# Score products as three float32r passes over halves, with the attention stage in a newly searched order

## The chip, the cores and the metric

The program runs on one core of one Trainium2 chip. The metric is the device time of one execution in microseconds. The kernel before takes 1178.76 us (median of 3 runs, 1177.21 to 1178.91).

## The reference

Attention over 4 x 8 heads of 576 positions with head size 64, where only scores within `tau` of a row's maximum count; then a gated layer on the 2304 x 512 result after RMS normalisation; then a second layer with `h * cos(h)`. Cut to what matters:

```python
scores = scale * np.matmul(q, k.transpose(0, 1, 3, 2))
thresh = np.max(scores, axis=-1, keepdims=True) - tau
scores = np.where(scores >= thresh, scores, -1000000000.0)
attn = np.exp(scores - np.max(scores, axis=-1, keepdims=True))
attn = attn / (np.sum(attn, axis=-1, keepdims=True) + 1e-09)
x = np.matmul(attn, v)                      # then to (2304, 512)

xn = x / np.sqrt(np.mean(x * x, -1) + 1e-06) * rms_g
g = xn @ w_gate
y = (silu(g) * (xn @ w_val)) @ w_out        # 512 -> 1536 -> 512
h = y @ w_in                                # 512 -> 2048
out = (h * np.cos(h)) @ w_out2              # 2048 -> 512
```

## The kernel before

**Three stages.** Attention works on 16 pairs of heads, the gated layer on 6 chunks of 384 tokens by 6 groups of 2 hidden blocks, the second layer on the same chunks by groups of 3 or 2. The two layers multiply in float32r: each operand is split into a rounded half (`hi`) and the remainder (`lo`), and `mm3` (L740) issues three matmuls, hi x hi, hi x lo and lo x hi, into one PSUM bank. Their order is written out in loops.

**A pair of heads in attention.** DMA brings k, q and v. `prep_pe` transposes k and q on TensorE (psb and psc for k, psa for q), `prep_act` copies them from PSUM to SBUF on ScalarE, q with the scale. Then five units follow, four of 128 queries for each of the two heads and a fifth that holds the last 64 queries of both. For a unit `s_mm` (L496) multiplies queries and keys into the PSUM tiles s0 and s1, of which each has one buffer; `s_max` copies them out on VectorE and takes the row extreme, `s_exp` is on ScalarE, `s_thr` on GpSimd, `s_mask` on VectorE, then `t_pe` (pst) and `c_pe` (psc) transpose the weights on TensorE, and `av` multiplies them with v (po). A pair's result is divided by the sums on GpSimd (`av_div`), squared and summed for the RMS (`x_sq`, `x_add`); after every fourth pair `x_sum` (pss, TensorE), `x_mean`, `rms` and `rms_t` make the RMS factor, which SP writes out and reads back spread over the partitions.

**The score products before.** The operands are plain float32. For units 0 to 3 a head's matmul uses 64 of the 128 rows of the array, head 0 the upper and head 1 the lower, so that the two heads' matmuls lie in different row groups; a unit is 2 column halves (288 columns each) x 2 heads, that is 4 matmuls in the program, and the trace shows 8, two for each float32 matmul. The fifth unit uses 64 x 64 tiles, 4 matmuls in the program and 8 in the trace.

**What sets the order.** Attention, with the first four blocks of gate and value products (`gv`, tile pgv) and the first two of output products (`px`) of the gated layer, is ordered by the class `Plan`: a list of steps with an engine, a duration, a place number (`STEPS`, L28), the steps that each follows, and the buffers that it takes and frees. `order` runs through it with one clock per engine and emits at each point the step that can start first by its durations, ties going to the place number. `SIGNAL` (L83) is added until another engine sees a step's end, `SWITCH` when TensorE changes its tile shape (`TILING`, L90). Each engine then works through its list strictly in that order, and so does SP with its DMAs. What comes after `plan.run` is a loop written out by hand; it begins with the third block of `px`, then block 4 of `gv`, and so on.

Of the kernel before, what the change touches and what calls it, by code (L numbers as in the profile page):

```python
# [10 lines left out]
F32R = mybir.dt.float32r  # L11
# [7 lines left out]
P = 128  # L19
# [9 lines left out]
    "none": ("", 0, 989236),  # L29
    "load_k": ("SP", 1700, -2080791, 5000),  # L30
    "load_q": ("SP", 1700, -71929, 7000),
    "load_v": ("SP", 1700, 1092105, 5000),
    "pb": ("PE", 440, -510840),
    "pa": ("PE", 440, -238233),
    "pc": ("PE", 330, 5527),
    "pb_a": ("ACT", 590, -16795),
    "pa_a": ("ACT", 690, -1741191),
    "pc_a": ("ACT", 480, -1089184),
    "s": ("PE", 960, -2067487),
    "s4": ("PE", 490, -536410),  # L40
    "warm": ("PE", 640, -512436),
    "max": ("DVE", 833, -2165065),
    "exp": ("ACT", 785, 18525),
    "th": ("POOL", 300, -79889),
    "mask": ("DVE", 890, -806542),
    "t": ("PE", 438, 45402),
    "raw": ("ACT", 595, -536576),
    "c0": ("PE", 220, -1677441),
    "c1": ("PE", 440, -448255),
    "c_raw": ("ACT", 415, -134803),  # L50
    "radd": ("POOL", 250, 59203),
    "rinv": ("DVE", 430, -724883),
    "r_out": ("SP", 2100, -470089, 2500),
    "r_in": ("SP", 1700, -1508061, 11000),
    "av0": ("PE", 2110, -2836787),
    "av1": ("PE", 2660, -1235121),
    "avo": ("ACT", 420, -1389171),
    "div": ("POOL", 1410, -632364),
    "xout": ("SP", 500, 133651, 2500),
    "sq": ("POOL", 1145, 981189),  # L60
    "x_add": ("POOL", 1410, 831228),
    "xsum": ("PE", 1150, 324869),
    "mean": ("DVE", 150, -1745391),
    "rms": ("POOL", 1520, 218301),
    "rs_out": ("SP", 2500, 1117322, 2500),
    "x_load": ("SP", 500, 404214, 6000),
    "x_p": ("POOL", 1010, 1534732),
    "x_a": ("ACT", 610, 636723),
    "x_d": ("DVE", 550, -11859),
    "jdma": ("SP", 500, 542601, 5000),  # L70
    "j1": ("DVE", 600, -1949661),
    "j2": ("DVE", 690, -1330761),
    "j_p": ("POOL", 1310, 3046632),
    "j_a": ("ACT", 620, -146518),
    "gv": ("PE", 2100, -1185087),
    "silu": ("ACT", 500, -877901),
    "px": ("PE", 2100, 184028),
    "pxc": ("ACT", 500, 1363803),
    "hmul": ("DVE", 560, 68682),
    "hhi": ("ACT", 520, -551420),  # L80
    "hlo": ("DVE", 560, -825852),
}
SIGNAL = 100  # L83
# [6 lines left out]
TILING = {"s": 1, "s4": 3, "av0": 2, "av1": 2}  # L90
# [15 lines left out]
class Plan:  # L106
# [8 lines left out]
    def add(self, kind, at, fn, *args, after=(), take=(), free=()):  # L115
        eng, ns, place, landing = (STEPS[kind] + (SIGNAL if STEPS[kind][0] else 0,))[:4]
# [95 lines left out]
def attention_moe_cos_kernel(  # L212
# [283 lines left out]
    def s_mm(n):  # L496
# [799 lines left out]
```

## Time and profile before

| | us |
|---|---|
| median of 3 runs | 1178.76 |
| the profiled execution | 1178.78 |
| its span | 1176.8 |
| attention up to the first block of pgv on TensorE | 304 |
| TensorE busy | 1162.3 |
| VectorE busy | 791.6 |
| ScalarE busy | 656.8 |
| GpSimd busy | 315.5 |

The profiled execution is within 0.02 us of the median, so that sums can be made against it; 2.0 us lie outside its span. In the profile PE is TensorE's matmuls, PEld its weight loads, DVE VectorE, ACT ScalarE, POOL GpSimd, SP the DMA queue. Matmuls are pipelined and overlap in the rows, so what a matmul costs the engine is read from start to start of the next one, not from its duration.

### The profile page before, as it was taken

What the parts mean: (1) busy time and instruction counts of PE and PEld (TensorE: products, weight loads), DVE (VectorE), ACT (ScalarE), POOL (GpSimd) and SP (SyncE); (2) the same over time, 40 slices, a digit from 0 to 9 for tenths busy, and PEclk for the clock granted to TensorE, in tenths of its full rate; (3) what the DMA queues carried; (4) which work ended last, traced back from release to release, by engine and by line L of the source; (5) the groups of instructions that cost most, each with busy time, mean ns of one, the idle gap of its engine ahead of it and who ended that gap; (6) DMA issues with size and microseconds to landing.
All of it is one profiled execution on the core that took longest, in us unless ns stands there. A gap on an engine that the chain in (4) does not pass through costs nothing.

```text
span 1176.8 us, 18220 instructions
## 1 busy us (share of the span) xinstructions
PE 1162.3 (99%) x6836; PEld 1021.4 (87%) x6836; DVE 791.6 (67%) x1547; ACT 656.8 (56%) x1234; POOL 315.5 (27%) x299
## 2 busy tenths in 40 slices
PE   9999999999999999999999999999999999999997
PEld 7666666666899999999999999999999999999995
DVE  6788777787477463643636439578687796867765
ACT  5888777776445321312313225377677676766663
POOL 1233343333653020100201102014234243332222
PEclk9999999999999999999999999999999999999999
DMA  6454324211543030110301103002112021000014
GB/s 134 118 146 113 89 70 102 56 51 49 152 160 105 19 108 1 54 55 1 108 1 54 54 1 91 18 1 75 34 36 72 1 72 36 27 11 1 1 54 108
DMA packets 99448, 71.66 MB, mean 61 GB/s; under 512 B 65040, under 2 KB 89360, under 8 KB 99360
## 3 DMA queue, kind: packets, MB, share of 16 engines
q1 hardware_dynamic: 98256, 70.20, 21.1%
q8 instruction: 54, 0.88, 0.3%
q10 hardware_dynamic: 1040, 0.26, 0.1%
q14 instruction: 34, 0.28, 0.1%
q0 software_dynamic: 64, 0.03, 0.0%
HBM read 60.95 MB, written 9.52 MB: 60 GB/s over the span
## 4 chain that ended last, share of the span: by engine, by line
PE 92%; issue 3%; ACT 2%; DVE 2%; DMA 0%; POOL 0%; SPq 0%; POOLq 0%; ACTq 0%
PE pgv L742 24%; PE ph L742 16%; PE po L742 16%; PE px L742 12%; PE s L510 8%; PE po L636 7%; PE pst L599 5%; ACT et L609 1%; PE psc L618 1%; PE psa L444 1%; ACT e L549 0%; PE psb L444 0%; PE pss L676 0%; PE warm L708 0%; DVE xl L736 0%
## 5 line engine op out<-in xcount | busy, mean ns | idle before, releaser
L742 PE MATMUL pgv<-xl,whi 128*128 128x384 f32 x576 | 194.5, 338 | 2.3 <-DVE xl L736 2.3
L742 PE MATMUL pgv<-xh,whi 128*128 128x384 f32 x576 | 194.4, 337 | 0.0
L742 PE MATMUL pgv<-xh,wlo 128*128 128x384 f32 x576 | 194.2, 337 | 0.0
L318 POOL TENSOR_TENSOR wtmp<-wtmp,raw 128x512 int32<-128x512 int32 x68 | 93.1, 1369 | 354.8 <-DVE wtmp L314 340.4
L1201 POOL TENSOR_TENSOR hlo<-r,hhi 128x384 fp32r<-128x384 f32 x96 | 98.2, 1023 | 303.6 <-ACT hhi L1200 247.6
L766 ACT ACTIVATE hh<-pgv 128x384 f32<-128x384 f32 x72 | 35.5, 493 | 248.8 <-PE pgv L742 248.8
L770 DVE TENSOR_TENSOR hh<-hh,pgv 128x384 f32<-128x384 f32 x72 | 39.7, 552 | 161.2 <-ACT hh L766 161.2
L742 PE MATMUL ph<-xh,whi 128*128 128x384 f32 x384 | 129.6, 337 | 0.0
L742 PE MATMUL ph<-xl,whi 128*128 128x384 f32 x384 | 129.5, 337 | 0.0
L742 PE MATMUL ph<-xh,wlo 128*128 128x384 f32 x384 | 129.2, 336 | 0.0
L530 DVE TENSOR_SCALAR_CACHE_REDUCE s<-s 128x576 f32<-128x576 f32 x128 | 91.9, 755 | 42.1 <-PE s L510 41.8
L1183 ACT ACTIVATE t<-ph,magic 128x384 f32<-128x384 f32 x96 | 55.8, 582 | 111.5 <-PE ph L742 111.5
L742 PE MATMUL po<-whi,hlo 128*128 128x512 f32 x288 | 114.6, 398 | 1.4 <-POOL hlo L1201 1.4
L742 PE MATMUL po<-whi,hhi 128*128 128x512 f32 x288 | 113.8, 395 | 0.2 <-ACT hhi L1200 0.2
L742 PE MATMUL po<-wlo,hhi 128*128 128x512 f32 x288 | 113.4, 394 | 0.0
L742 PEld LDWEIGHTS pgv<-xl,whi 128*128 128x128 f32 x576 | 108.6, 189 | 3.0 <-DVE xl L736 2.9
L742 PEld LDWEIGHTS pgv<-xh,whi 128*128 128x128 f32 x576 | 108.7, 189 | 0.6 <-issue 0.5
L742 PEld LDWEIGHTS pgv<-xh,wlo 128*128 128x128 f32 x576 | 108.7, 189 | 0.0
L559 DVE SCALAR_TENSOR_TENSOR e<-s,th,e 128x576 f32<-128x576 f32 x128 | 101.0, 822 | 0.5 <-POOL th L540 0.4
L1190 DVE SCALAR_TENSOR_TENSOR r<-t,r 128x384 f32<-128x384 f32 x96 | 99.0, 1032 | 3.3
L549 ACT ACTIVATE e<-s,m 128x576 f32<-128x576 f32 x128 | 95.2, 785 | 4.9 <-DVE s L530 4.8
L742 PE MATMUL px<-hhi,whi 128*128 128x384 f32 x288 | 97.9, 340 | 0.0
(118 smaller groups left out, 2456.5 us busy)
## 6 DMA issues: line engine op xcount, KB each, us to landing
raw<-in_moe_w_out_dram SPq DMA_DIRECT2D x28, 512.0 KB
raw<-in_moe_w_in_dram SPq DMA_DIRECT2D x16, 512.0 KB
raw<-in_moe_w_gate_dram SPq DMA_DIRECT2D x12, 512.0 KB
raw<-in_moe_w_val_dram SPq DMA_DIRECT2D x12, 512.0 KB
x<-xb SPq DMA_DIRECT2D x16, 288.0 KB
kn<-in_k_dram SPq DMA_DIRECT2D x16, 256.0 KB
vn<-in_v_dram SPq DMA_DIRECT2D x16, 256.0 KB
qn<-in_q_dram SPq DMA_DIRECT2D x15, 256.0 KB
```

The lines of the kernel that those rows point to most:

```text
L318: nc.gpsimd.tensor_tensor(tmp, tmp, lw, op=ALU.add)
L510: nc.tensor.matmul(ps[:, c, 0:288], lhs, kh[r, k0:k0 + 288], start=True, stop=True,)
L530: nc.vector.tensor_scalar(s.rearrange("p (c n) -> p c n", c=2), un[n].pop(("ps", hd))[:, :, 0:288], qscale[:, 0:1] if n % 5 == 4 else 1.0, ...
L549: nc.scalar.activation(un[n]["e"][:, hd], un[n]["s", hd], AF.Exp, bias=grp[group_of(n)]["m"][:, c], scale=-1.0)
L559: nc.vector.scalar_tensor_tensor(e, un[n].pop(("s", hd)), grp[group_of(n)]["th"][:, ci:ci + 1], e, op0=ALU.is_le, op1=ALU.mult, accum_out= ...
L599: nc.tensor.transpose(ps[:, c], e[:, hd, k0:k0 + P], ident)
L636: nc.tensor.matmul(po[64 * hd:64 * hd + 64, :], vn[:, c, hd, :] if c < 4 else vl[:, hd, :], hf[j]["et"][:, hd, c, :] if c < 4 else hf[j][" ...
L742: nc.tensor.matmul(ps, w[a], x[bb], start=first and i == 0, stop=last and i == 2)
L770: nc.vector.tensor_tensor(hq[n], hq[n], pgv.pop(n)[:, 1, 0:TC], op=ALU.mult)
L1183: nc.scalar.activation(t, ph, AF.Identity, bias=magic[:, 0:1], scale=INV2PI)
L1190: nc.vector.scalar_tensor_tensor(r, t, -C2, r, op0=ALU.mult, op1=ALU.add)
L1201: nc.gpsimd.tensor_tensor(lo, r, f(hi), op=ALU.subtract)
```

## The change

The score products go from float32 to three float32r passes. `prep_act` now writes the rounded half of q and k; a new step `prep_lo` on VectorE (pa_l, pb_l, pc_l) computes the remainder from the same PSUM tile, three instructions for each pair; `s_mm` runs three passes for each column half: 12 matmuls for units 0 to 3, in alternating row groups as before. The fifth unit is no longer cut into 64 x 64 tiles: the last 64 queries of the two heads are loaded as a block-diagonal 128 x 128 tile, which takes two DMAs instead of one in `load_q`, and one matmul over all 128 rows gives both heads; it has 6 matmuls and TensorE's usual tile shape. There are two tiles each of k and q (a hi and a lo one) where four could be held before. The first unit waits for pair 0's `prep_lo` too.

In the engine model the durations of `STEPS` are new throughout, `SIGNAL` is set for each engine, `s4` has left `TILING`, and the place numbers are new, so that the order of the whole attention stage is another. The instructions after that stage are the same ones in the same order, from the third block of `px` on.

```diff
-    "s": ("PE", 960, -2067487),
-    "s4": ("PE", 490, -536410),
...
+    "pb_l": ("DVE", 605, -2192168),
...
+    "s": ("PE", 885, -3334861),
+    "s4": ("PE", 790, 52577),
...
-SIGNAL = 100
+SIGNAL = {"PE": 190, "DVE": 110, "ACT": 145, "POOL": 60, "SP": 100, "": 0}
...
-TILING = {"s": 1, "s4": 3, "av0": 2, "av1": 2}
+TILING = {"s": 1, "av0": 2, "av1": 2}
...
-        small(p).dma_start(
-            q4[p % 2][0:64].rearrange("p (h d) -> p h d", h=2), rest(q, p).rearrange("h p d -> p h d")
-        )
+        for j in range(2):
+            r = slice(64 * j, 64 * j + 64)
+            small(p).dma_start(q4[p % 2][r, r], rest(q, p)[j])
...
-            qk[nm, p] = f(qk_p.tile([P, w], F32R, tag=nm + ("hi", "lo")[p % 2], name=nm))
+            qk[nm, p] = [qk_p.tile([P, w], F32R, tag=nm + x, name=nm + x) for x in ("hi", "lo")]
...
+    def prep_lo(p, kind):
+        nm = "q" if kind == "a" else "k"
+        c0, c1 = PREP_COLS[kind]
+        hi, lo = (x[:, c0:c1] for x in qk[nm, p])
+        nc.vector.scalar_tensor_tensor(
+            lo, pre.pop((p, kind))[:, 0:c1 - c0], qscale[:, 0:1] if kind == "a" else 1.0, f(hi),
+            op0=ALU.mult, op1=ALU.subtract,
+        )
...
         for c in range(2):
-            for hd in range(2):
-                k0 = 288 * c + (64 if hd and u < 4 else 128)
-                r = slice(64 * hd, 64 * hd + 64)
-                if u == 4:
-                    ps, lhs = un[n]["ps", 0][r], kh[r, 768:832]
-                else:
-                    ps, lhs = un[n]["ps", hd], qk["q", p][r, u * P:(u + 1) * P]
-                nc.tensor.matmul(
-                    ps[:, c, 0:288], lhs, kh[r, k0:k0 + 288], start=True, stop=True,
-                )
+            for i, (a, bb) in enumerate(((0, 0), (0, 1), (1, 0))):
+                for hd in heads(n):
+                    k0 = 288 * c + (64 if hd else 128)
+                    r = slice(0, P) if u == 4 else slice(64 * hd, 64 * hd + 64)
+                    lhs = kh[a][:, 768:896] if u == 4 else qk["q", p][a][r, u * P:(u + 1) * P]
+                    nc.tensor.matmul(
+                        un[n]["ps", hd][:, c, 0:288], lhs, kh[bb][r, k0:k0 + 288],
+                        start=i == 0, stop=i == 2,
+                    )
...
-            "s0": 1, "s1": 1, "t": 3, "v": 1, "k": 4, "q": 4, "kn": 2, "qn": 2, "q4": 2, "vn": 2,
+            "s0": 1, "s1": 1, "t": 3, "v": 1, "k": 2, "q": 2, "kn": 2, "qn": 2, "q4": 2, "vn": 2,
...
-                    ready[p].append(add("p" + kind + "_a", n, prep_act, p, kind, after=[x],
+                    x = add("p" + kind + "_a", n, prep_act, p, kind, after=[x])
+                    ready[p].append(add("p" + kind + "_l", n, prep_lo, p, kind, after=[x],
                         free=[("pre", p, kind)],
                     ))
```

**Where instructions now stand.** First TensorE, in the sixth pair, the last two units: s_ tiles are the score products of head 0 and head 1, pst the transposes of the weights. Before:

```order
217 L510 MATMUL s_1490<-k,q 128x288
218 L510 MATMUL s_1491<-k,q 128x288
219 L510 MATMUL s_1490<-k,q 128x288
220 L510 MATMUL s_1491<-k,q 128x288
221 L599 MATMUL pst<-ident,e 128x128 x8
222 L510 MATMUL s_1517<-k 64x288 x4
```

Now (L520 is the line of the score products, khi, klo, qhi and qlo are the halves; the six matmuls of the unit's first column half stand ahead of these, and three more of the last unit behind):

```order
423 L520 MATMUL s_1671<-khi,qhi 128x288
424 L520 MATMUL s_1672<-khi,qhi 128x288
425 L520 MATMUL s_1671<-klo,qhi 128x288
426 L520 MATMUL s_1672<-klo,qhi 128x288
427 L520 MATMUL s_1671<-khi,qlo 128x288
428 L520 MATMUL s_1672<-khi,qlo 128x288
429 L610 MATMUL pst<-ident,e 128x128 x12
430 L520 MATMUL s_1722<-khi 128x288
431 L520 MATMUL s_1722<-klo,khi 128x288
432 L520 MATMUL s_1722<-khi,klo 128x288
```

The unit of two heads has gone from 4 rows to 12, the fifth unit from 4 rows of 64 x 288 to 6 of 128 x 288, between the same neighbours.

Next VectorE, round the fifth unit's maximum (with qscale) of the third pair; L530 and L541 are the maxima, L559 and L570 the masks, L328 and L331 a weight's low half. Before:

```order
68 L530 TENSOR_SCALAR s,m<-s_787 128x576
69 L530 TENSOR_SCALAR s,m<-s_788 128x576
70 L530 TENSOR_SCALAR s,m<-s_831,qscale 128x576
71 L571 RECIPROCAL r_145<-r_145 128x9
72 L572 STREAM_TRANSPOSE rt<-r_145 128x32
73 L559 SCALAR_TENSOR_TENSOR e,sum<-s,th,e 128x576
74 L328 TENSOR_TENSOR wlo<-wtmp,whi 128x512
75 L559 SCALAR_TENSOR_TENSOR e,sum<-s,th,e 128x576
76 L530 TENSOR_SCALAR s,m<-s_874 128x576
```

Now:

```order
82 L541 TENSOR_SCALAR s,m<-s_944,qscale 128x576
83 L331 TENSOR_TENSOR wlo<-wtmp,whi 128x512
84 L487 SCALAR_TENSOR_TENSOR klo<-psb,khi 128x512
85 L487 SCALAR_TENSOR_TENSOR qlo<-psa,qscale,qhi 128x512
86 L541 TENSOR_SCALAR s,m<-s_987 128x576
87 L541 TENSOR_SCALAR s,m<-s_988 128x576
88 L487 SCALAR_TENSOR_TENSOR klo<-psc,khi 128x384
89 L570 SCALAR_TENSOR_TENSOR e,sum<-s,th,e 128x576
90 L541 TENSOR_SCALAR s,m<-s_1029 128x576
91 L541 TENSOR_SCALAR s,m<-s_1030 128x576
92 L570 SCALAR_TENSOR_TENSOR e,sum<-s,th,e 128x576
```

The three remainders of the next pair's keys and queries (L487) have come in between the maxima.

Last the end of attention. On GpSimd xe is chunk 1 of the next layer's input being scaled, acc chunk 3, and r_149 the power that gives the last RMS factor. Before:

```order
131 L667 TENSOR_TENSOR sq<-sq 128x576
132 L729 TENSOR_TENSOR xe<-xe 128x384 x4
133 L795 TENSOR_TENSOR acc<-acc,rs 128x1536
134 L687 TENSOR_TENSOR r_149<-r_149,expo 128x5
135 L318 TENSOR_TENSOR wtmp<-wtmp,raw 128x512
```

Now:

```order
131 L678 TENSOR_TENSOR sq<-sq 128x576
132 L740 TENSOR_TENSOR xe<-xe 128x384 x4
133 L698 TENSOR_TENSOR r_149<-r_149,expo 128x5
134 L806 TENSOR_TENSOR acc<-acc,rs 128x1536
135 L321 TENSOR_TENSOR wtmp<-wtmp,raw 128x512
```

The power (L687, now L698) stands ahead of the scaling of chunk 3 (L795, now L806), behind which it stood. TensorE at the same place, where pss is the sum of squares for that factor and px the first blocks of output products; before:

```order
700 L742 MATMUL px_4078<-hhi,whi 128x384
701 L742 MATMUL px_4078<-hlo,whi 128x384
702 L742 MATMUL px_4078<-hhi,wlo 128x384
703 L676 MATMUL pss<-ones,sq 128x1 x5
704 L742 MATMUL px_4174<-hhi,whi 128x384
```

Now:

```order
1275 L753 MATMUL pgv<-xh,whi 128x384
1276 L753 MATMUL pgv<-xl,whi 128x384
1277 L753 MATMUL pgv<-xh,wlo 128x384
1278 L687 MATMUL pss<-ones,sq 128x1 x5
1279 L753 MATMUL px_4736<-hhi,whi 128x384
```

The sum stood behind the 24 matmuls of the first two blocks of px and now stands ahead of them, right behind the fourth block of pgv. The last two po steps, which before stood ahead of all pgv, now stand between the second and the third block.

## Rows read from the trace of the kernel before

**Rows 1.** Page, part 1: busy time of each engine, share of the span, instructions.
```profile
PE 1162.3 (99%) x6836; PEld 1021.4 (87%) x6836; DVE 791.6 (67%) x1547; ACT 656.8 (56%) x1234; POOL 315.5 (27%) x299
```

**Rows 2.** Busy us (x instructions) in attention: PE, PEld, DVE, ACT, POOL; clock, DMA.
```profile
20.00:304.00 284.00, 281.19 (x2107) 186.48 (x2103) 223.21 (x614) 221.32 (x402) 102.57 (x116) 1.00 0.35 92
```

**Rows 3.** Waits within 20 to 304: engine line <- releaser, us in total, times, longest.
```profile
DVE s L530 <- PE s L510: 53.2, 65, 2.7
...
PEld s L510 <- DVE e L559: 9.0, 23, 0.5
```

**Rows 4.** PE timeline, unit of undivided queries: start, us, line, tile, xcount.
```profile
151.44 1.24 PE L510 MATMUL s<-k,q 64*128 64x288 f32 x8
152.62 0.44 PE L618 MATMUL psc<-ident,e 128*128 128x128 f32 x2
152.89 0.27 PE L449 MATMUL psb<-ident,k 128*128 128x128 f32 x1
153.00 0.49 PE L444 MATMUL psb<-ident,kn 128*128 128x128 f32 x3
```

**Rows 5.** PE timeline, fifth unit (64 x 64 tiles), and what stands round it.
```profile
165.04 0.60 PE L599 MATMUL pst<-ident,e 128*128 128x128 f32 x4
165.57 1.19 PE L510 MATMUL s<-k 64*64 64x288 f32 x8
166.69 0.49 PE L636 MATMUL po<-et,vn 128*64 128x320 f32 x2
```

**Rows 6.** Weight loads (PEld) and matmuls of one such step, in three windows.
```profile
151.79 0.19 PEld L510 LDWEIGHTS s<-k,q 64*128 64x128 f32 x2
...
152.03 0.19 PEld L510 LDWEIGHTS s<-k,q 64*128 64x128 f32 x2
...
151.79 0.65 PE L510 MATMUL s<-k,q 64*128 64x288 f32 x4
```

**Rows 7.** Groups by line: DVE operations on PSUM and SBUF; xcount, busy us, mean ns.
```profile
L1241 DVE TENSOR_TENSOR acc<-acc,po 128x512 f32<-128x512 f32 x90 | 60.9, 685 | 28.7 <-PE po L742 28.1
...
L1189 DVE SCALAR_TENSOR_TENSOR r<-t,ph 128x384 f32<-128x384 f32 x96 | 52.8, 550 | 61.1 <-ACT t L1184 60.4 <-ACT hhi L1200 0.7
```

**Rows 8.** PE timeline, float32r matmuls of 384 and 512 columns.
```profile
900.93 0.33 PE L742 MATMUL ph<-xh,whi 128*128 128x384 f32 x1
...
901.45 0.40 PE L742 MATMUL po<-whi,hhi 128*128 128x512 f32 x1
...
903.55 0.34 PE L742 MATMUL ph<-xh,whi 128*128 128x384 f32 x1
```

**Rows 9.** DVE's busiest 20 us of attention at a full PE, by stretch.
```profile
80.00:100.00 20.00, 19.96 (x148) 13.15 (x146) 17.28 (x46) 16.37 (x31) 8.34 (x10) 1.00 0.53 141
```

**Rows 10.** PE timeline, first unit of the program: start, us, what, releaser.
```profile
8.39 1.24 PE L510 MATMUL s<-k,q 64*128 64x288 f32 x8 [0.50 <-ACT q L476]
```

**Rows 11.** PE timeline, end of attention's steps and the stall behind it.
```profile
325.17 1.17 PE L676 MATMUL pss<-ones,sq 128*128 128x1 f32 x10
...
354.23 0.43 PE L742 MATMUL pgv<-xh,whi 128*128 128x384 f32 x1
356.43 0.44 PE L742 MATMUL pgv<-xl,whi 128*128 128x384 f32 x1 [1.76 <-DVE xl L736]
```

**Rows 12.** Stretch behind that stall, columns as in the group by stretch above.
```profile
357.10:360.50 3.40, 3.40 (x12) 3.40 (x12) 2.82 (x6) 1.44 (x3) 0.00 (x0) 0.50 0.00 0
```

**Rows 13.** POOL and DVE timelines there: chunk 3 scaled, the power, chunk 4 split.
```profile
326.31 3.50 POOL L795 TENSOR_TENSOR acc<-acc,rs 128x1536 f32<-128x1536 f32 x1
329.76 1.51 POOL L687 TENSOR_TENSOR r<-r,expo 128x5 f32<-128x5 f32 x1
...
355.77 2.19 DVE L736 SCALAR_TENSOR_TENSOR xl<-acc,g_sb,xh 128x384 fp32r<-128x384 f32 x4
```

**Rows 14.** DVE and POOL: the last mask, and the last sum of squares.
```profile
296.65 0.81 DVE L559 SCALAR_TENSOR_TENSOR el<-s,th,el 128x576 f32<-128x576 f32 x1
...
319.31 1.43 POOL L667 TENSOR_TENSOR sq<-sq 128x576 f32<-128x576 f32 x1 [0.82 <-DVE hlo L778]
```

More of the change, by code (lines that the diff above doesn't have):

```diff
@@ L43 @@
[L43 to L81, printed above, removed]
+    "none": ("", 0, 42756),
+    "load_k": ("SP", 1700, -6287439, 5000),
+    "load_q": ("SP", 2300, -583941, 7000),
@@ new lines @@
+    "load_v": ("SP", 1700, 266270, 5000),
+    "pb": ("PE", 440, -860938),
+    "pa": ("PE", 440, -872284),
+    "pc": ("PE", 355, 39154),
+    "pb_a": ("ACT", 477, -1117404),
+    "pa_a": ("ACT", 580, -2512624),
+    "pc_a": ("ACT", 362, -2064268),
+    "pa_l": ("DVE", 605, -2991832),
+    "pb_l": ("DVE", 605, -2192168),
+    "pc_l": ("DVE", 470, -5857582),
+    "s": ("PE", 885, -3334861),
+    "s4": ("PE", 790, 52577),
+    "warm": ("PE", 640, 30908),
+    "max": ("DVE", 680, -4929605),
+    "exp": ("ACT", 675, 1243882),
@@ new lines @@
+    "th": ("POOL", 300, -873324),
+    "mask": ("DVE", 742, -1254623),
+    "t": ("PE", 445, 69130),
+    "raw": ("ACT", 477, -1893158),
+    "c0": ("PE", 245, -2814656),
+    "c1": ("PE", 465, 3616),
+    "c_raw": ("ACT", 295, -1313205),
+    "radd": ("POOL", 250, -463947),
+    "rinv": ("DVE", 375, -2021598),
+    "r_out": ("SP", 2100, -3188116, 2500),
+    "r_in": ("SP", 1700, -348085, 11000),
+    "av0": ("PE", 2212, -5925497),
+    "av1": ("PE", 2745, -2855374),
+    "avo": ("ACT", 300, -133807),
@@ new lines @@
+    "div": ("POOL", 1385, 1088743),
+    "xout": ("SP", 500, 2391295, 2500),
+    "sq": ("POOL", 1122, 1869781),
+    "x_add": ("POOL", 1385, 1123049),
+    "xsum": ("PE", 1085, 246324),
+    "mean": ("DVE", 140, -2146351),
+    "rms": ("POOL", 1520, 1629785),
+    "rs_out": ("SP", 2500, 2224996, 2500),
+    "x_load": ("SP", 500, 2392020, 6000),
+    "x_p": ("POOL", 1010, 1606859),
+    "x_a": ("ACT", 540, 3436637),
+    "x_d": ("DVE", 480, -40858),
+    "jdma": ("SP", 500, 2917392, 5000),
+    "j1": ("DVE", 440, -3496085),
@@ L82 @@
+    "j2": ("DVE", 608, -2428094),
+    "j_p": ("POOL", 1310, 2858989),
+    "j_a": ("ACT", 540, 290309),
+    "gv": ("PE", 2090, -400213),
+    "silu": ("ACT", 420, 2761497),
+    "px": ("PE", 2090, 288516),
+    "pxc": ("ACT", 400, -194883),
+    "hmul": ("DVE", 480, -472662),
+    "hhi": ("ACT", 420, 1595094),
+    "hlo": ("DVE", 480, -4555793),
 }
-SIGNAL = 100
+SIGNAL = {"PE": 190, "DVE": 110, "ACT": 145, "POOL": 60, "SP": 100, "": 0}
 SWITCH = 100
@@ L115, in add @@
     def add(self, kind, at, fn, *args, after=(), take=(), free=()):
-        eng, ns, place, landing = (STEPS[kind] + (SIGNAL if STEPS[kind][0] else 0,))[:4]
+        eng, ns, place, landing = (STEPS[kind] + (SIGNAL[STEPS[kind][0]],))[:4]
         step = {
@@ L852, in attention @@
             prep_act(0, kind)
+            prep_lo(0, kind)
             warm(m)
```

18 lines of the change are left out of this document (3 added, 15 removed).

## Prediction

> **What bounds the kernel now.** The page's first part comes first: TensorE is busy for 99% of the span, VectorE for 67% [rows 1]. Since matmuls overlap in the rows, that share alone proves little, so the stretch of attention comes next: from 20 to 304 us TensorE is busy for 281.2 of 284 us at the full clock, VectorE for 223.2, ScalarE for 221.3 [rows 2]. The list of waits then tells which way the waiting goes: VectorE sits idle for 53.2 us until a score product has ended, while the largest wait of TensorE's weight loads, for a mask on VectorE, comes to 9.0 us in 23 pieces [rows 3]. So attention runs at TensorE's pace, and what a step costs TensorE from start to start counts nearly one for one. The new order ends there too: what follows is the same list of instructions, so nothing but its start and one stall at its beginning can move.
>
> **The score products of two heads.** A unit starts at 151.44 and the next instruction at 152.62, 1.18 us [rows 4]. A transpose in a row takes 0.11 us (152.89 to 153.00) [rows 4]; four of them from 165.04 should end at 165.48, yet the next unit starts at 165.57, so a change of tile shape costs 0.09 us ahead of the step [rows 5]. That makes 1.27 us for a unit. Inside it, one pair of float32 instructions (both heads at once) follows the next at 0.24 us, 151.79 to 152.03 [rows 6]; four pairs are 0.96 us, and 0.31 us are edges, the first weight load and the draining for the other tile shape. The new unit keeps the edges and has 6 pairs in float32r.
>
> A float32r pass of 288 columns is not in the trace. Three of 384 columns take 0.52 us from 900.93 to 901.45, 0.173 each, and nine of 512 take 2.10 us up to 903.55, 0.233 each [rows 8]: 0.451 and 0.456 ns for a column, so proportional, and 0.130 us for 288. The bounds: a pass cannot be cheaper than half a float32 pair, 0.120, and is not dearer than the one of 384 columns, 0.173. I take 0.130, which both sizes give. A unit then costs 6 x 0.130 + 0.31 = 1.09 us, 0.18 less, and 16 x 4 units give 11.5 us.
>
> The Trainium skill, "TensorE: Matmul & The Clock Gate", section "Back-to-back issue gap", states N/2.4 + 2.5 ns for a matmul in a stream. By that a pass would be 122.5 ns, as an estimate, and the whole sum below would come to about 1160.7 us; for 384 columns it says 162.5 ns where the row shows 173, so the trace does not agree.
>
> That the two heads still run at once in float32r is an assumption, and the rows that carry it are those of float32: the loads of both heads are in one piece of 0.19 us at 151.79, x2, in the moment in which the matmuls of the pair before start, 151.79 [rows 6]. Neither the other row group nor a matmul in flight holds the load back.
>
> The same page, Part 3, "The mechanism", says that a weight load overlaps a matmul in flight only where the row group differs; here it would put a load between any two passes. The trace does not agree: the load at 151.79 belongs to the same two row groups as the matmuls that start at 151.79.
>
> **The fifth unit.** It runs from 165.57 to 166.69, 1.12 us, with 0.09 ahead [rows 5], so 1.21. The new one has 6 passes over the full array and TensorE's usual tile shape, so no edges: 0.78 us, 0.43 less, and 6.9 us for 16 pairs. Together TensorE is relieved of **18.4 us**. With passes of 0.120 it would be 23, with 0.173 it would be 2.4 us more work than before.
>
> **What VectorE gets.** Three remainders for each pair, each from PSUM and SBUF. The nearest rows are 685 ns for 512 columns and 550 ns for 384 [rows 7], so 2 x 0.685 + 0.55 = 1.92 us a pair, 28.8 us for the 15 pairs that are prepared behind 20 us. They lie beside TensorE's work as long as they fall into the 53.2 us in which VectorE waits for score products [rows 3]. But s0 and s1 have one buffer each: the next unit's products wait for this unit's maxima, and a remainder that stands ahead of a maximum, as it now does, puts it off by 0.55 to 0.69 us. VectorE's share rises from 79% to about 252 of 271 us, 93%; the highest that I find in 20 us beside a full TensorE is 17.28, 86% [rows 9]. The bounds are nothing and all 28.8 us. I take 5 us, nearer to the lower end, because the idle time is nearly twice the new work and TensorE's waits for VectorE are now only a few us; about one remainder in six then reaches TensorE.
>
> **The beginning.** The first unit starts at 8.39, when ScalarE has written pair 0's operands [rows 10]. Now its last remainder comes behind that, 0.55 us with the row of 384 columns. TensorE waits there for the chain of one unit, so the relief of the first five units and the first fifth one, 5 x 0.18 + 0.43 = 1.3 us, is not on the path either. Together **1.9 us** against the change. The second small load of q4 costs SP or POOL one more issue; the loads run a pair ahead, and I cost it at nothing. If that cover is gone, it is under 1 us for each pair. Two k and q tiles instead of four mean that a pair is prepared right behind the last unit of the pair two before it, still a whole pair (some 17 us) ahead of its use; I cost that at nothing too.
>
> **The end of attention.** The sum for the last RMS factor, pss, starts at 325.17 [rows 11], and chunk 4 of the next layer, which needs the factor, is split from 355.77 on [rows 13]; TensorE waits for it from 354.23 to 356.43 [rows 11], 2.0 us beyond the pace of 0.17. Behind that stall the granted clock is at half, 1.2 GHz, from 357.1 to 360.5 [rows 12], 3.4 us for the work of 1.7. In the new order pss stands ahead of 24 px matmuls (24 x 0.173 = 4.2 us), and the power, 1.51 us, no longer waits for the scaling of chunk 3, 3.50 us [rows 13]. The chain is 7.7 us earlier against TensorE's list, more than the stall, so 3.7 us should go. A new wait may come at pss itself: from the last mask, over at 297.46, to the last sum of squares, over at 320.74 [rows 14], are 23.3 us, with a round trip through DRAM in it, and between them TensorE now has four blocks of pgv (16.6 us), 12 transposes (1.3 us) and two po steps, which is about as much. I take 0.7 us of the 3.7 back and count **3.0 us**.
>
> **The sum,** against the profiled execution of 1178.8, which is also the median: 1178.8 - 18.4 + 1.9 + 5 - 3.0 = **1164.3 us**.
>
> **Rivals.**
> - VectorE becomes the bound. If it cannot be filled beyond the 86.4% of [rows 9], 252 us of work need 252/0.864 = 291.7 us, 7.7 more than the 284 of now: 1178.8 + 7.7 + 0.6 - 3.0 = 1184 us, slower than before. It decides below a share of 252/(284 + 2.4) = 88%. For it speaks that maxima and masks come in bursts and that ScalarE and VectorE work in turns on each unit; against it that VectorE's idle time now is TensorE's doing [rows 3].
> - The heads no longer run at once in float32r. A unit has 12 passes, 1.87 us, 0.60 more: 64 x 0.60 - 6.9 = 31.5 us more, and 1178.8 + 31.5 + 1.9 - 3.0 = 1209 us. If each pass first waited for its load of 0.19 us, a unit would take 6 x 0.32 + 0.31 = 2.23 us and a fifth unit 1.92, 64 x 0.96 + 16 x 0.71 = 72.8 us more, 1250 us in all. Against both stands [rows 6]. (The second is what the rule of Part 3 above would give.)
> - A smaller gain: VectorE costs 12 us instead of 5, or the stall behind attention stays since TensorE waits at pss instead. 1171 and 1167 us, 1174 for both.
> - A larger gain: passes at 0.120 and the wait for VectorE at nothing, 1155 us. (The skill's rule on the gap points this way.)
>
> **How the numbers follow.** About 0.2%, 2.4 us, is what a measurement of this kernel can tell from no change. Chances: 0.60 for the forecast with its own spread of 1157 to 1170; 0.06 for less than that; 0.13 for the smaller gain, 1170 to 1176; 0.06 for within 2.4 us of now; 0.11 for VectorE as the bound and 0.04 for heads one after the other or loads between the passes. That is 0.79 faster, 0.06 the same, 0.15 slower. The range from 1156 to 1180 leaves out both slower rivals and the end of the larger gain, some 0.2.
>
> **What would show it.** In the new profile a unit of two heads should take about 1.0 us from its first matmul to the next instruction, its pairs 0.13 us apart with both heads within 0.01; a fifth unit 0.78 us. If the pairs are 0.26 apart, the second rival holds. VectorE's share of attention should be 90% or more, and TensorE's wait for L541 and L570 some us in total; if attention's part of TensorE's list ends no earlier, the first rival holds. The first pgv of chunk 4 should follow without a stall and the clock should stay at its full level there; a wait at pss would show as idle time ahead of it, for GpSimd's last sum.

## The result

The changed kernel takes **1166.64 us** (median of 4 runs, 1164.42 to 1167.45) against 1178.07 before (4 runs, 1177.21 to 1178.91): a ratio of 0.9904, 95% interval 0.9892 to 0.9916, 11.4 us less. A second group of runs on another occasion gave 1165.91 against 1177.81, 0.9896 (0.9882 to 0.9911). The forecast was 1164.3. The direction, the size and the relief by the products of two heads came out as worked out. The fifth unit's relief was taken too large and the price of VectorE's new work too high, and the two errors nearly cancel. One execution below, of the kernel with one pass, took 2758.64 us, more than twice the others of that kernel, and is left out of its median.

The profiled execution took 1167.45 us with a span of 1165.6. Its page, part 1 (busy us, share of the span, instructions) and part 4 (the chain that ended last, by engine and by line), answer to [rows 1]:

```profile
PE 1145.0 (98%) x7060; PEld 1036.4 (89%) x7060; DVE 817.5 (70%) x1595; ACT 653.2 (56%) x1234; POOL 317.4 (27%) x300
...
PE 86%; DVE 7%; issue 4%; ACT 1%; POOL 1%; DMA 0%; SPq 0%; POOLq 0%; DVEq 0%; ACTq 0%
PE pgv L753 24%; PE ph L753 16%; PE po L753 16%; PE px L753 12%; PE po L647 5%; PE s L520 5%; PE pst L610 4%; DVE s L541 2%; DVE e L570 2%; PE psc L629 1%; DVE klo L487 1%; DVE wtmp L317 0%; DVE wtmp L312 0%; PE pss L687 0%; DMA k<-in_k_dram 0%
```

TensorE is busy 17 us less. VectorE has a larger part of the chain than any engine but TensorE: the maxima (L541), the masks (L570) and the new remainders (L487) stand in it.

Attention by stretch (length, then busy us of PE, PEld, DVE, ACT, POOL; clock, DMA), answering to [rows 2], and the waits from 20 to 288 us, answering to [rows 3]:

```profile
20.00:288.00 268.00, 260.05 (x2266) 199.12 (x2265) 248.79 (x658) 215.30 (x397) 100.08 (x112) 0.99 0.38 98
```
```profile
DVE s L541 <- PE s L520: 12.5, 22, 1.9
PEld s L520 <- DVE s L541: 7.4, 18, 1.4
PE s L520 <- DVE s L541: 4.0, 8, 1.1
```

The first pgv starts at 288.23 instead of 304.01, but that is not the same point: 12 transposes and two po steps, 7.1 us from 296.67 to 303.79, now stand behind the second block. The first mark with the same work ahead of it in both kernels is block 4 of `gv`. Before, then the changed kernel in this trace:

```profile
328.37 0.34 PE L742 MATMUL pgv<-xh,whi 128*128 128x384 f32 x1
```
```profile
319.74 0.34 PE L753 MATMUL pgv<-xh,whi 128*128 128x384 f32 x1
```

It starts 8.6 us earlier here, and 11.6 in a second trace, which has not the half clock shown below. VectorE is busy for 248.79 of 268 us, 93%, and its wait for score products has fallen from 53.2 to 12.5 us. TensorE's loads now wait for maxima for 7.4 us and its matmuls, partly in the same pieces, for 4.0; in [rows 3] the largest such wait, for masks, was 9.0.

A unit of two heads on TensorE (start, us, line, tile, count), answering to [rows 4 and 6]:

```profile
100.36 0.40 PE L520 MATMUL s<-khi,qhi 64*128 64x288 f32 x2
100.59 0.30 PE L520 MATMUL s<-klo,qhi 64*128 64x288 f32 x2
100.73 0.29 PE L520 MATMUL s<-khi,qlo 64*128 64x288 f32 x2
100.86 0.29 PE L520 MATMUL s<-khi,qhi 64*128 64x288 f32 x2
101.00 0.30 PE L520 MATMUL s<-klo,qhi 64*128 64x288 f32 x2
101.13 0.29 PE L520 MATMUL s<-khi,qlo 64*128 64x288 f32 x2
101.35 0.33 PE L629 MATMUL psc<-ident,e 128*128 128x128 f32 x1
```

It takes 0.99 us from its first matmul to the next instruction, with 0.09 ahead 1.08. Each row holds both heads, 3 to 4 ns apart, and behind the first pair, which takes 0.23, the pairs follow each other at 0.13 to 0.14 us. A fifth unit, answering to [rows 5]:

```profile
111.59 0.38 PE L520 MATMUL s<-khi 128*128 128x288 f32 x1
111.80 0.29 PE L520 MATMUL s<-klo,khi 128*128 128x288 f32 x1
...
112.34 0.29 PE L520 MATMUL s<-khi,klo 128*128 128x288 f32 x1
112.47 0.60 PE L610 MATMUL pst<-ident,el 128*128 128x128 f32 x4
```

It takes 0.88 us: its first pass lasts 0.21 until the next one starts, not 0.13.

The stall behind attention, answering to [rows 11 and 13]. First TensorE, then POOL and DVE in the same microseconds:

```profile
344.78 0.43 PE L753 MATMUL pgv<-xh,whi 128*128 128x384 f32 x1
346.97 0.44 PE L753 MATMUL pgv<-xl,whi 128*128 128x384 f32 x1 [1.77 <-DVE xl L747]
```
```profile
342.03 3.81 POOL L806 TENSOR_TENSOR acc<-acc,rs 128x1536 f32<-128x1536 f32 x1
...
342.42 3.98 DVE L331 TENSOR_TENSOR wlo<-wtmp,whi 128x512 fp32r<-128x512 f32 x1
...
346.31 2.19 DVE L747 SCALAR_TENSOR_TENSOR xl<-acc,g_sb,xh 128x384 fp32r<-128x384 f32 x4
```

The stall has not gone: 2.19 us from start to start, where [rows 11] has 2.20. The forecast said that it would go.

A half clock that the trace of before has not is at the beginning (same columns as the stretch above; the clock is the last number but two), behind a wait of TensorE for a remainder:

```profile
25.00:33.00 8.00, 6.79 (x37) 4.81 (x39) 6.67 (x15) 2.95 (x6) 1.95 (x2) 0.57 0.61 138
```
```profile
24.35 0.27 PE L467 MATMUL psc<-ident,q 128*128 128x128 f32 x1
26.21 0.69 PE L610 MATMUL pst<-ident,e 128*128 128x128 f32 x2 [1.59 <-DVE qlo L487]
```

Three questions followed. What do the passes and the fifth unit give, each by itself? What do the remainders cost, and how near is VectorE to being the bound? And what holds the two stalls?

### The profile page after: what moved, and what is told of

Read it like the earlier page. It is cut to its first block, busy times and chain, and to the rows that moved or that the text cites. A ratio compares the mean times of both kernels' runs of the same rounds, so it can differ in the third digit from the quotient of the medians.

```text
span 1165.6 us, 18659 instructions
## 1 busy us (share of the span) xinstructions
PE 1145.0 (98%) x7060; PEld 1036.4 (89%) x7060; DVE 817.5 (70%) x1595; ACT 653.2 (56%) x1234; POOL 317.4 (27%) x300
## 4 chain that ended last, share of the span: by engine, by line
PE 86%; DVE 7%; issue 4%; ACT 1%; POOL 1%; DMA 0%; SPq 0%; POOLq 0%; DVEq 0%; ACTq 0%
PE pgv L753 24%; PE ph L753 16%; PE po L753 16%; PE px L753 12%; PE po L647 5%; PE s L520 5%; PE pst L610 4%; DVE s L541 2%; DVE e L570 2%; PE psc L629 1%; DVE klo L487 1%; DVE wtmp L317 0%; DVE wtmp L312 0%; PE pss L687 0%; DMA k<-in_k_dram 0%
## 5 line engine op out<-in xcount | busy, mean ns | idle before, releaser
L570 DVE SCALAR_TENSOR_TENSOR e<-s,th,e 128x576 f32<-128x576 f32 x128 | 104.5, 846 | 1.4 <-POOL th L551 1.2
L560 ACT ACTIVATE e<-s,m 128x576 f32<-128x576 f32 x128 | 96.0, 796 | 12.7 <-DVE s L541 12.6
L541 DVE TENSOR_SCALAR_CACHE_REDUCE s<-s 128x576 f32<-128x576 f32 x128 | 91.6, 752 | 10.8 <-PE s L520 10.6
```

Source lines behind the costliest of these rows:

```text
L541: nc.vector.tensor_scalar(s.rearrange("p (c n) -> p c n", c=2), un[n].pop(("ps", hd))[:, :, 0:288], qscale[:, 0:1] if n % 5 == 4 else 1.0, ...
L560: nc.scalar.activation(un[n]["e"][:, hd], un[n]["s", hd], AF.Exp, bias=grp[group_of(n)]["m"][:, c], scale=-1.0)
L570: nc.vector.scalar_tensor_tensor(e, un[n].pop(("s", hd)), grp[group_of(n)]["th"][:, ci:ci + 1], e, op0=ALU.is_le, op1=ALU.mult, accum_out= ...
```

## Experiments

All kernels are the changed one with one edit. Unless it is said otherwise, the order of the instructions is that of the changed kernel, and differences are against its second group of runs, 1165.91 us.

**What TensorE's relief is worth.** Two runs undo one part each. The first makes all score products in float32 again, of the rounded halves alone, and leaves the fifth unit undivided:

```diff
-            for i, (a, bb) in enumerate(((0, 0), (0, 1), (1, 0))):
+            for i, (a, bb) in enumerate(((0, 0),)):
...
-                    lhs = kh[a][:, 768:896] if u == 4 else qk["q", p][a][r, u * P:(u + 1) * P]
+                    lhs = f(kh[a][:, 768:896]) if u == 4 else f(qk["q", p][a][r, u * P:(u + 1) * P])
...
-                        un[n]["ps", hd][:, c, 0:288], lhs, kh[bb][r, k0:k0 + 288],
+                        un[n]["ps", hd][:, c, 0:288], lhs, f(kh[bb][r, k0:k0 + 288]),
```

> The order, the remainders and everything else of the changed kernel, but each score product is again one float32 product (of the rounded halves, so the low halves are left out), two heads at once; the fifth unit stays undivided. Theory A (TensorE's work sets the pace, so the passes count nearly one for one): a unit takes 1.27 instead of 1.09 us, 64 x 0.18 = 11.5, a fifth unit 2 x 0.48 instead of 0.78, 16 x 0.18 = 2.9, and the idle pieces shrink by up to 3 us: 1177 to 1180, so the gain of the change is nearly all in the passes and the fifth unit. Rival (the gain is in the order, with 34 changes of tile shape fewer, and VectorE hides the passes): below 1172.

Measured: 1178.51 us (11 runs), a ratio of 1.0002 to the kernel before (0.9994 to 1.0011). That is 12.6 us more than the changed kernel, within Theory A. In its trace a fifth unit takes 0.97 us, so the work put back is 64 x 0.18 + 16 x 0.09 = 13.0 us. New order, remainders and an undivided fifth unit together are worth nothing without the passes.

The second divides the fifth unit alone again:

```diff
+                if u == 4:
+                    if i:
+                        continue
+                    for hd in range(2):
+                        r = slice(64 * hd, 64 * hd + 64)
+                        nc.tensor.matmul(
+                            un[n]["ps", 0][r, c, 0:288], f(kh[0][r, 768 + 64 * hd:832 + 64 * hd]),
+                            f(kh[0][r, 288 * c + 128:288 * c + 416]), start=True, stop=True,
+                        )
+                    continue
```

> One part alone undone: the fifth unit again in quarters of 64 by 64 in float32 (the low halves are left out of these products only), everything else as in the changed kernel. Theory A (sum of the prediction, a fifth unit is 0.41 us shorter in the trace and TensorE sets the pace): 16 x 0.41 = 6.6 us more, 1172.5. Rival (behind a fifth unit TensorE waits for VectorE anyway): 3 us more or less, up to 1169.5.

Measured: 1171.48 us, ratio 0.9947 (0.9935 to 0.996), 5.6 us more. The expectation had 0.41 us for a fifth unit (the prediction 0.43); with the 0.88 us of the trace a fifth unit is (1.12 + 0.09) - 0.88 = 0.33 us shorter, 16 x 0.33 = 5.3 us, which is near what the run shows. Theory A's mechanism holds at this lower price.

**What the remainders cost.** One run cuts them to 8 columns, and the products no longer read the low halves:

```diff
-            for i, (a, bb) in enumerate(((0, 0), (0, 1), (1, 0))):
+            for i, (a, bb) in enumerate(((0, 0), (0, 0), (0, 0))):
...
-            lo, pre.pop((p, kind))[:, 0:c1 - c0], qscale[:, 0:1] if kind == "a" else 1.0, f(hi),
+            lo[:, 0:8], pre.pop((p, kind))[:, 0:8], qscale[:, 0:1] if kind == "a" else 1.0, f(hi[:, 0:8]),
```

> The three remainders of each pair on VectorE cut to 8 columns, and all three passes made with the rounded halves alone (the low halves are left out of the products), order and all other instructions as in the changed kernel. Theory A (the remainders on VectorE cost what the trace shows as new idle time of TensorE: 6.8 us up to 100 us, the beginning with it, about 1.2 us at 220 to 260 and up to 3 us of half clock behind the first of them): 8 to 11 us less, 1156 to 1159. Theory B (the prediction's sum: 5 and 1.9 us): 7 us less, 1159.7. Rival (TensorE's work alone sets the pace, the idle pieces are of the new order): no more than 2 us less, 1164.6 or above.

Measured: 1162.57 us, ratio 0.9867 (0.9852 to 0.9882), only 3.3 us less. Both my theories were too high, and the rival at 2 us too low. The cut is not one to nothing, as the lengths (least, median and most in ns) of the short remainders show:

```profile
L487 DVE SCALAR_TENSOR_TENSOR klo<-psb,khi x16: 154/162/167, 7.8 to 248.6; 128x8 fp32r<-128x8 f32 x16
L487 DVE SCALAR_TENSOR_TENSOR qlo<-psa,qscale,qhi x16: 210/224/228, 8.4 to 249.2; 128x8 fp32r<-128x8 f32 x16
L487 DVE SCALAR_TENSOR_TENSOR klo<-psc,khi x16: 152/160/168, 8.8 to 251.9; 128x8 fp32r<-128x8 f32 x16
```

A pair takes 0.55 us instead of 1.98 (0.69, 0.74 and 0.55 in the changed kernel), so that 21.5 of the 29.7 us for 15 pairs go, and a quarter stays. The rows of the stretch from 20 to 275 us, ahead of the first pgv in all of them (PE, PEld, DVE, ACT, POOL), before, the changed kernel in its second run, and this one:

```profile
20.00:275.00 255.00, 253.23 (x1908) 168.87 (x1905) 201.67 (x557) 202.03 (x366) 90.31 (x102) 1.00 0.35 91
```
```profile
20.00:275.00 255.00, 247.11 (x2182) 189.11 (x2181) 239.14 (x634) 205.89 (x380) 96.84 (x108) 1.00 0.37 97
```
```profile
20.00:275.00 255.00, 249.19 (x2208) 192.33 (x2205) 224.91 (x640) 208.21 (x386) 96.87 (x108) 1.00 0.37 98
```

TensorE's idle time is 1.8, 7.9 and 5.8 us, so of the 6.1 us that the change added there, 2.1 go with three quarters of the remainders' work. Nearly all of the 6.1 lies in the first quarter, from 20 to 84 us: before, with short remainders, and with the float32 products of the first experiment (the changed kernel's row stands further below, under another order):

```profile
20.00:84.00 64.00, 63.14 (x478) 42.85 (x475) 52.08 (x139) 54.03 (x99) 18.87 (x23) 1.00 0.52 130
```
```profile
20.00:84.00 64.00, 59.09 (x518) 44.75 (x517) 57.48 (x163) 52.99 (x99) 20.49 (x24) 1.00 0.53 136
```
```profile
20.00:84.00 64.00, 59.05 (x422) 39.88 (x421) 59.13 (x153) 50.50 (x92) 18.67 (x23) 1.00 0.50 130
```

TensorE is idle there for 0.9 us before, 6.6 in the changed kernel, 4.9 with short remainders, and 5.0 with whole remainders at TensorE's old pace. So neither the length of the remainders nor TensorE's pace makes most of it; what the last three have in common is the new order. Idle time is not the whole price, though: by the mark of block 4 of `gv`, 313.28 here and 316.77 in the changed kernel's second run, at a full clock in both, the cut gives back 3.5 us.

**How near VectorE is.** The opposite edit writes every remainder twice:

```diff
+        nc.vector.scalar_tensor_tensor(
+            lo, pre[p, kind][:, 0:c1 - c0], qscale[:, 0:1] if kind == "a" else 1.0, f(hi),
+            op0=ALU.mult, op1=ALU.subtract,
+        )
```

> Every remainder on VectorE is written twice, 28.8 us more work there for the 15 pairs behind the first. Theory A (VectorE has 19 us left and its work comes in bursts): 12 to 20 us more, 1178 to 1186, so VectorE would be the bound. Rival (the price is the one that cutting the remainders short showed, 3.3 us for 28.8 us): 3 to 5 us more, 1169 to 1171.

Measured: 1202.46 us, ratio 1.0206 (1.019 to 1.0221): 36.5 us more, twice what Theory A allowed, for 30.0 us of work (the second writing takes 0.69, 0.75 and 0.56 us a pair in its trace). Two rows of its trace, for 20 to 60 and for 100 to 200 us:

```profile
20.00:60.00 40.00, 34.11 (x263) 25.25 (x263) 35.76 (x85) 26.18 (x48) 5.73 (x8) 0.87 0.39 95
...
100.00:200.00 100.00, 95.39 (x807) 70.79 (x805) 94.93 (x241) 75.16 (x138) 37.40 (x40) 0.98 0.35 90
```

VectorE is at 95% in the long stretch, and TensorE, which now waits for it, falls to the half clock in places (0.87 on average from 20 to 60 us). That is how the price can exceed the work; how much of it is the clock was not measured.

From the other side, one run takes work from TensorE:

```diff
-            for i, (a, bb) in enumerate(((0, 0), (0, 1), (1, 0))):
+            for i, (a, bb) in enumerate(((0, 0),)):
...
-                        start=i == 0, stop=i == 2,
+                        start=i == 0, stop=True,
```

> Only the first of the three passes is left (the two with a low half are left out), remainders and order as in the changed kernel. It takes 64 x 4 x 0.130 + 16 x 4 x 0.130 = 41.6 us of work from TensorE. Theory A (VectorE stands close behind TensorE: 19 us idle of the 268 between 20 and 288 us): no more than 15 to 20 us less, 1146 to 1151, and VectorE busy for 98% there. Rival (the first rival of the prediction is far off, VectorE has room): 35 us less or more, 1131 or below.

Measured: 1158.80 us (median of three runs, 1157.71 to 1160.46), 7.1 us less for 41.6 us of work: far from the rival, and less than even Theory A's 15. The same kernel ran again for its trace:

> The kernel with one pass (the two with a low half left out) once more, for its trace. Theory A (VectorE holds it): in the 240 us from 20 us on VectorE is busy for 96% or more, TensorE's idle time stands behind maxima and remainders of VectorE, and part of it is followed by a half clock. Rival (the chain within a unit or ScalarE holds it): VectorE below 93% there, as in the changed kernel, and waiting itself for score products or ScalarE.

Measured: 1159.32 us. The stretch from 20 to 260 us, and the waits in it:

```profile
20.00:260.00 240.00, 219.08 (x1587) 151.09 (x1586) 231.30 (x606) 201.96 (x370) 91.32 (x103) 0.96 0.39 100
```
```profile
PEld s L520 <- DVE s L541: 18.4, 45, 1.7
...
PE s L520 <- DVE s L541: 7.4, 18, 1.4
...
DVE s L541 <- PE s L520: 3.0, 4, 1.2
```

VectorE is busy for 96.4%, TensorE for 91%; VectorE waits for score products for 3.0 us, TensorE's loads for maxima for 18.4. Theory A holds: VectorE is the bound in this stretch, and the clock's mean of 0.96 takes a further part.

Then both edits at once, one pass and short remainders:

> Both at once: only the first of the three passes (the two with a low half are left out), and the remainders on VectorE cut to 8 columns. Theory A (VectorE held the run with one pass, which took 41.6 us from TensorE and gained only 7): with 28.8 us less on VectorE it now gains 20 to 30 us more, 1130 to 1139. Rival (ScalarE, the chain within a unit, or the clock held it): within 8 us of the run with one pass, 1152 to 1159.

Measured: 1145.13 us (1142.48 to 1146.91), 13.7 us less than with one pass alone. That lies between the two theories. Of the 21.5 us that the cut takes from VectorE 13.7 count here, against 3.3 beside three passes, so VectorE did hold the run with one pass, but it did not do so alone.

**The two stalls.** The wait at 26.2 us was filled with seven matmuls on a constant:

```diff
+            if p == 1:
+                one = ones.broadcast_to([P, P])
+                for i in range(7):
+                    nc.tensor.matmul(ps[:, 384:512], one, one, start=True, stop=True)
```

> Seven matmuls of 128 columns on a constant, 1.5 us, put into the idle piece of 1.6 us ahead of the transposes at 26.2 us, where TensorE waits for the remainder qlo of VectorE; they write columns of that bank that nobody reads. Theory A (the half clock from 25.4 us on follows from this idle piece together with the other small ones before it, and costs about 3 us): the clock stays full there and every run takes about 1164.4 us, 2 to 3 us less than the changed kernel's median of 1166.6. Rival (the whole thin beginning lowers the clock, whatever stands in this one gap): the episode stays and the median remains at 1166.6.

The changed kernel itself ran beside it:

> The changed kernel itself, once more, beside the others of this batch. The trace of the first run shows the clock at half for 6.8 us from 25.4 us on, and the runs with a mean granted clock of 1.0 and 0.996 took 1164.4 and 1167.3 us. Theory A (the half clock at the beginning comes and goes from run to run and costs about 3 us): the times fall between 1164.3 and 1167.5 and follow the mean clock. Rival (the spread is something else, a transfer for instance): times differ by as much at equal mean clock.

Measured: 1165.54 and 1165.91 us; nothing to tell apart. Filling the gap did not do what Theory A said: three of the four runs still took 1165.3 us or more, at a mean clock of 0.997. In both traces the clock from 25 to 33 us is full, with the gap and without it. Of the eight runs of the changed kernel, the two with a mean clock of 1.00 took 1164.4 and 1164.5 us, the six with 0.996 to 0.998 took 1165.9 to 1167.5, so a lower mean clock goes with 1.4 to 3 us a run. The two traces of the changed kernel show the upper end: block 4 of `gv` starts at 319.74 us with the half clock at the beginning and here, in the second run without it, 2.97 us earlier:

```profile
316.77 0.34 PE L753 MATMUL pgv<-xh,whi 128*128 128x384 f32 x1
```

But it isn't tied to the one gap. In the run with short remainders of the same batch it stood behind the stall of pgv:

```profile
340.00:345.00 5.00, 4.46 (x17) 4.35 (x18) 4.42 (x9) 2.51 (x6) 0.00 (x0) 0.68 0.01 3
```

What decides in which run and behind which gap the clock falls is left open.

For the stall of pgv the scaling of a chunk on GpSimd was cut in four:

```diff
-        nc.gpsimd.tensor_tensor(
-            acc[c], acc[c], xrs[c][:, None, :].broadcast_to([P, KD, TC]), op=ALU.mult
-        )
+        for kk in range(KD):
+            nc.gpsimd.tensor_tensor(acc[c][:, kk], acc[c][:, kk], xrs[c], op=ALU.mult)
```

> The scaling of a chunk by its RMS factors on GpSimd, one operation of 1536 columns (3.8 to 4.0 us), written as four of 384. Theory A (the stall of 1.8 us at 346.97 is the shared port of VectorE and GpSimd: the split of weights on VectorE, L331, 0.7 us by itself, takes 3.98 us beside the scaling of chunk 5, and the remainders xl of chunk 4 stand behind it): VectorE gets in between the pieces, the stall goes, 1.5 to 2.0 us less, about 1164.8. Theory B (the prediction's: the stall waits for the RMS factor, pss or the power): the stall stays, 1166.6.

Measured: 1164.48 us, 1.4 us less; the intervals of the two ratios (0.9872 to 0.9902 here) overlap, so the trace has to decide. First VectorE's split of weights (L331) in the changed kernel's second run, then this kernel:

```profile
339.42 3.99 DVE L331 TENSOR_TENSOR wlo<-wtmp,whi 128x512 fp32r<-128x512 f32 x1
```
```profile
336.96 1.79 DVE L331 TENSOR_TENSOR wlo<-wtmp,whi 128x512 fp32r<-128x512 f32 x1
...
339.47 4.74 DVE L747 SCALAR_TENSOR_TENSOR xl<-acc,g_sb,xh 128x384 fp32r<-128x384 f32 x4 [0.71 <-issue]
339.88 5.19 POOL L807 TENSOR_TENSOR acc<-acc,rs 128x384 f32<-128x384 f32 x4
...
344.26 0.45 PE L753 MATMUL pgv<-xl,whi 128*128 128x384 f32 x1 [0.49 <-DVE xl L747]
```

VectorE now gets through beside the pieces of chunk 4's scaling, so the same split L331 begins 2.5 us earlier, takes 1.79 us instead of 3.99, and is over before the scaling of chunk 5 begins at 339.88. The remainders of chunk 4 now run beside the pieces, slowly (4.74 us for four, where [rows 13] have 2.19), and the longest stall of that block is 0.83 us from start to start instead of 2.2. So the stall was this: while GpSimd scales chunk 5 in one operation, VectorE's split of weights does not end, and the remainders that TensorE waits for are queued behind it. The RMS factor comes when it came before (GpSimd begins to scale chunk 4 at 331.61 us here, at 331.70 in the changed kernel), and yet the stall shrinks. Theory A holds, but for a rest of the stall.

**Another order.** What stayed open were the 4 to 5 us of idle time from 20 to 84 us that neither the length of the remainders nor TensorE's pace explains. Two other tables of places were made for the same instructions; two lines of the first, in which the other places are new as well:

```diff
-    "j1": ("DVE", 440, -3496085),
-    "j2": ("DVE", 608, -2428094),
+    "j1": ("DVE", 440, -1901676),
+    "j2": ("DVE", 608, -1030690),
```

(j1 and j2 are VectorE's steps on the weights, which now come later against the others.) Both also have the scaling in four pieces.

> The changed kernel with other places in the table, so another order of the same instructions in attention, found with the same step times, and with the scaling of a chunk in four pieces as in the run before. The table's own account puts the last TensorE step of attention's part 9.5 us earlier than in the changed kernel. Theory A (the 8.8 us of idle pieces that TensorE gained up to 300 us belong to the order, above all to the bursts on VectorE between 60 and 84 us, and not to the remainders as such): 6 to 10 us below the run with the scaling in pieces (1164.5), 1155 to 1158. Rival (VectorE's total is what holds, any order leaves such pieces): 2 us below it at most, 1162.5 or above.

Measured: **1155.06 us** (1154.88 to 1155.37), ratio 0.9807 (0.9792 to 0.9822), 9.4 us less than with the scaling in pieces alone and 10.9 less than the changed kernel. Theory A holds. The stretches from 20 to 84 and 84 to 275 us, first of the changed kernel in its second run, then of this one:

```profile
20.00:84.00 64.00, 57.41 (x497) 42.99 (x496) 60.73 (x157) 50.86 (x94) 18.95 (x24) 1.00 0.50 129
84.00:275.00 191.00, 189.70 (x1688) 146.11 (x1686) 178.41 (x478) 155.03 (x287) 77.89 (x85) 1.00 0.33 86
```
```profile
20.00:84.00 64.00, 63.09 (x562) 48.26 (x561) 63.02 (x167) 53.57 (x99) 19.51 (x22) 1.00 0.44 110
84.00:275.00 191.00, 190.35 (x1699) 145.53 (x1697) 185.17 (x491) 160.39 (x297) 80.69 (x89) 1.00 0.37 99
```

The larger part of the difference is in the first 64 us: TensorE is idle for 0.9 us there instead of 6.6, and both engines are at 98% or more. That is 5.7 of the 8.9 us by which block 4 of `gv` starts earlier than in the kernel with the scaling in pieces (307.73 and 316.67). So the idle time belonged to the order: all remainders are in place here. Which of the new places does it is not shown. In the changed kernel VectorE has 14 operations of weight jobs from 20 to 84 us, 8.4 us, and in the new order four, all ahead of 60 us; but the kernel before had 12 there, 7.2 us, with hardly any idle time.

> A second table of places, found from another start, otherwise as the kernel beside it; by the table's account the last TensorE step comes 10.6 us earlier than in the changed kernel, with the first px block ahead of the last two gv blocks. Theory A: 7 to 10 us below 1164.5, 1154 to 1157.5; if the late gv blocks make the next px block wait, 2 us of it go. Rival as beside it: 1162.5 or above.

Measured: 1160.83 us, ratio 0.9858 (0.9841 to 0.9874), 3.7 us below the run with the scaling in pieces: between the two theories. Its last px block came too early for what it needs:

```profile
305.48 0.34 PE L753 MATMUL px<-hhi,whi 128*128 128x384 f32 x1
309.52 0.69 PE L753 MATMUL px<-hlo,whi 128*128 128x384 f32 x1 [3.71 <-DVE hlo L789]
```

That is 3.9 us beyond the pace of 0.17, where I had allowed for 2, and the mean clock from 300 to 320 us is 0.91. A table that is better by its own account can lose the gain just behind the part that it accounts for.

## Why the prediction came out as it did

- **What bounds the kernel.** Right: 13.0 us of work put back on TensorE cost 12.6 us.
- **Two heads at once in float32r.** Right in each part: pairs 0.13 us apart, the heads within 0.01, the loads never in between (those of the second pair start at 100.46, 0.13 ahead of its matmuls and beside the pair before), 1.08 us for a unit where I had 1.09. The relief of 11.5 us stands, and the rivals with heads one after the other or loads between passes are out. The Trainium skill's rule of N/2.4 + 2.5 ns ("TensorE: Matmul & The Clock Gate", "Back-to-back issue gap") gives 122.5 ns for a pass, as an estimate; that section gives it as the gap of an isolated matmul and other figures for a stream, so I took it for more than it says, and the pairs here are 130 to 140 ns apart.
- **The fifth unit.** Mis-sized: 0.88 us and not 0.78. I gave it no edges since it keeps TensorE's usual tile shape, but its first pass takes 0.21 us. The term is 5.3 us, not 6.9, and the relief 16.8, not 18.4.
- **VectorE's remainders, 5 us, and the beginning, 1.9.** Mis-sized: block 4 of `gv` starts 11.6 us earlier at the full clock, so of the relief of 16.8 all of VectorE's new work, the new order and the beginning together take 5.2 us, not 6.9. The ratio "about one remainder in six reaches TensorE" is near what the cut shows, 3.5 of 21.5 us. How the 1.7 us that are left divide is not shown.
- **What the sum left out.** The step that set 28.8 us of work against the 53.2 us of waits of the whole attention was too coarse: of the 6.1 us of new idle time from 20 to 275 us, 5.7 lie from 20 to 84. About 4 of them stay with short remainders and with the old pace of TensorE, and go in another order with the remainders whole, so they belong to the order, for which the sum has no term there. With the 3.5 us of the remainders that is more than the 5.2 us of the mark, so if these prices add up, the new order gives some 2 us back elsewhere; where, no run shows.
- **VectorE as the bound, the rival on the other side.** Its cap of 86.4% was wrong: VectorE runs at 93% here and at 98% from 20 to 84 us in the other order, beside a full TensorE. It was nearer than its chance of 0.11 says, though: 30.0 us more on VectorE cost 36.5, and 41.6 us less on TensorE gain 7.
- **The end of attention, 3.0 us.** The wait at pss did not come: pss starts at 312.22 right behind pgv, and px at 313.25. But the stall stayed, since I took its releaser from the order of events (factor, load, split) and not from what VectorE was doing: an operation that takes 0.7 us elsewhere lasted 3.98 beside GpSimd. What went is the half clock behind it, which comes and goes, and 0.8 us between block 4 of `gv` and the stalled matmul (28.06 us before; 27.22 in the second run, from 316.77 to 343.99). From there to the end of the span it is 820.4 us before and 818.6 now, 1.8 less. That is 2.6 us where I had 3.0, but the 2.0 us of the stall itself are not among them.

Put together: 1178.8 less 16.8, plus 5.2, less 0.8 and 1.8, is 1164.6, and the second run's profiled execution, at the full clock up to its last microseconds, took 1164.5. The 5.2 is itself what the traces leave over, so this sum proves nothing by coming out; it shows how the forecast's terms compare: a relief 1.6 us too large stands against a price 1.7 us too high. That the forecast lies within 0.2 us of that execution is luck in the sizes, on a mechanism that was right. The medians of 1166.6 and 1165.9 lie above it because most runs have a half clock somewhere, for which the sum has no term.

## What to carry to other kernels

When work moves from the engine that is the bound to one with idle time, look at the idle time stretch by stretch, after the change too: a mean share of 79% for VectorE said nothing of where TensorE would wait, and nearly all of its new idle time lay in the first 64 us. Another order took that away without touching the work. Here, with two engines above 90%, relieving either alone gained little (41.6 us less on TensorE 7, 21.5 less on VectorE 3.3), and the order of the work was worth as much as the work: the change gave 11 us, and a better order of the same instructions 9 more. And name the releaser of a stall from what the waiting engine's neighbours run in those microseconds, not from the chain of data alone.

## What the runs showed of the hardware

- Two float32r matmuls of 64 rows each, in the two row groups, start 3 to 4 ns apart, and the loads of a pair run beside the pair before it, in the same row groups.
- VectorE operations that take 0.69 us (L331) and 0.42 us (L312) by themselves lasted 3.98 and 3.73 us when GpSimd ran an operation of 1536 columns, 3.81 and 3.95 us long, beside them. Remainders xl, 0.55 us each in [rows 13], took 1.2 us each beside pieces of 384 columns.
- Behind the same waits of 1.6 to 1.8 us the granted clock fell to half in one trace and not in another: in the changed kernel's first trace for 6.8 us behind the wait at 26 us, in its second behind neither that wait nor the stall of pgv, and before behind the stall of pgv, for 3.4 us.
- The first float32r pass behind transposes of the same tile shape takes 0.21 us, the following ones 0.13 to 0.14.
- A remainder of 8 columns still takes 0.16 to 0.22 us on VectorE; one of 384 or 512 columns takes 0.55 to 0.74.
